# A fused RWKV attention and mixing kernel: the first batch's MLP in runs of three and six steps, with new places for late weights and for the second batch's preparation

## The chip, the cores and the metric

The kernel runs on one core of one Trainium2 chip. The metric is the device time of one launch, in microseconds (us). The kernel before took 422.9 us, the median of three runs (422.41 to 423.47). The engines are called by the profile's names: PE (TensorE), DVE (VectorE), ACT (ScalarE), POOL (GpSimd) and SP (SyncE, which issues most DMAs here).

## The reference

The first half is a linear attention with a decaying state, for 4 batches and 8 heads over 768 tokens of 48 numbers each. The second half mixes over tokens (rank 32) and then over channels (384 to 1536 and back).

```python
for t in range(S):                                   # attention, per batch and head
    cur = einsum('bhd,bhe->bhde', u * k[t], v[t])
    y[t] = einsum('bhd,bhde->bhe', r[t], state + cur)
    state = w * state + einsum('bhd,bhe->bhde', k[t], v[t])
x = y.transpose(0, 2, 1, 3).reshape(4, 768, 384)
h = x.transpose(0, 2, 1) @ U @ V                     # U: 768 x 32, V: 32 x 768
u = x + h.transpose(0, 2, 1)
out = u + maximum(u @ w_ch1, 0) @ w_ch2              # w_ch1: 384 x 1536, w_ch2: 1536 x 384
```

U, V, w_ch1 and w_ch2 arrive as float64 and are turned into float32 on the chip, bit by bit. Each 32-bit factor of the MLP is then split into a high part (a cast to the fp32r type) and a low part (what the cast lost), and a product is three matmuls: high by high, low by high, high by low.

## The kernel before, in words

**Attention by chunks.** The four batches of 768 tokens are 24 chunks of 128 tokens, six to a batch: n = 0 to 5 are batch 0, 6 to 11 batch 1, and so on. A chunk needs its r, k, v (loads `ld`, `vsw`; for some chunks of batches 1 to 3 `bl`, blocks of r and k in pieces of 128 bytes, line 686), then `ks`, transposes with decay factors (`rT`, `kT`), `dv` and `dg` (r times k times u, and its sum), which together are called its preparation. Then it goes through PE (`pab`, `pav`) and the carried state (`S`, `SW`), and line 896 adds the result up as `x_n`, a tile of 128 tokens by 384 channels.

**G and u^T.** G = U^T x needs all six x of a batch. For batch 0 it is gathered in the PSUM bank `wake` (`c_gx`), and `c_g0` copies it to SBUF: the high part by ACT (`Gs_0`, line 951), the low part by DVE (line 952). Then u, transposed, is made in two blocks of 384 tokens (t = 0 and 1) by `c_xu`: PE transposes x into banks `pu` and adds V^T G; ACT casts the high part `uTh` (line 1034), DVE subtracts the low part `uTl` (line 1035).

**The MLP by steps.** A step (t, f) is one token block and one of 12 slices of 128 hidden channels. `m_1` multiplies u^T by slice f of W1 (nine matmuls into bank `mm`, of which there is one); ACT makes relu and cast (`hr`, line 1103, and `hh`), an engine the low part (`hl`, line 1105). `m_2` multiplies by slice f of W2 (nine matmuls into three banks `acc`, one for each 128 tokens, called `p2`). The half steps go m_1 of step i, then m_2 of step i - 1. The first step of a block with f = 0 puts three "gates" ahead (`p<-Gs,V`: G by V, the part of u that is not x). At the end of a run of steps with one t, DVE adds the three `p2` to the x tiles (line 1143), which frees the banks for the next run; once all 12 slices are added, x is stored. Batch 0 goes through three runs before the change: t 0 with f 0 to 5, t 1 with f 0 to 11, t 0 with f 6 to 11. The other batches have two: t 0 and t 1 with all 12.

**The weights.** Every slice of W1 or W2 is a "unit" (`w1_f`, `w2_f`): a load of 384 KB (line 512, on SP), a byte instruction that picks out the upper exponent bits (line 533 on DVE or 537 on ACT), a scaling on ACT (line 559), sign and join on DVE (lines 540 and 543), the high part on ACT (line 577) and the low part on POOL or DVE (line 578). Batch 0 decodes them all; the results stay for the other batches.

**The order.** A planner in the kernel (`Plan`) writes the order of every engine's queue. Each operation has a due time (its key, given by `at(t, ...)`), an estimated cost, what it reads and writes (`Buf`), and rings of buffers by tag. The planner goes forward in estimated time, gives an engine the operation with the earliest key of those that it thinks ready, and chooses between engines where an operation has alternatives. On the chip each engine then works its queue in that order; waits are put in by the real reads and writes. In gaps that the planner foresees on PE it puts filler matmuls (`wake`, `wake2`). Due times are set by constants: `T0` = 46 (the start of batch 0's MLP in the planner's time), `PER` = 1.95 a half step, `FRONT` = 9 and `EACH` = 5.5 for the chunks of batch 0, `LEAD` = 12 (how long before its use a weight is loaded), `EARLY` = 4 (weights loaded ahead of the rest).

## Time and profile before

| | before |
|---|---|
| median of three runs | 422.9 us (422.41 to 423.47) |
| the profiled execution | 422.63 us, of which the span is 420.9 us |
| mean granted clock of PE | 0.991 |
| PE busy | 402.0 us (96%) |
| PE weight loads | 388.6 us (92%) |
| DVE busy | 280.6 us (67%) |
| ACT busy | 188.1 us (45%) |
| POOL busy | 75.6 us (18%) |
| HBM read, written | 37.95 MB, 8.26 MB |

The span runs from the first to the last instruction of the profiled execution, and all positions below are microseconds from its start. Busy is the time with an instruction in work. A row of a timeline shows the start, how long the group took, the engine, the line, the operation, its tiles and shape and how many instructions stand in it; a bracket at its end gives an idle time ahead of it and what ended it. A row of the stretches shows the stretch and its length, then for PE, PE's weight loads, DVE, ACT and POOL the busy time and in brackets the instructions, then the granted clock of PE (1.00 is full speed), the share of time in which the DMA engines worked and the rate in GB/s.

### The profile page before, as it was taken

The numbers are of one execution on the slowest core, as the hardware profiler recorded it, in microseconds if no ns is written. First come the engines' busy times: TensorE is split into PE (matmuls) and PEld (weight loads), VectorE is DVE, ScalarE is ACT, GpSimd is POOL, SyncE is SP. The second block draws the span as 40 slices with busy tenths as digits, with TensorE's granted clock in tenths as the row PEclk, the third lists the DMA queues.
The fourth block names the chain that finished last, engine by engine and source line by source line (L and its number), as shares of the span: only waits on it lengthen the run. The fifth ranks groups of instructions, "written<-read, shape, count | busy, mean of one in ns | idle before, by whom it ended". The sixth has DMA issues, their size and how long they took to land.

```text
span 420.9 us, 12333 instructions
## 1 busy us (share of the span) xinstructions
PE 402.0 (96%) x5111; PEld 388.6 (92%) x5111; DVE 280.6 (67%) x620; ACT 188.1 (45%) x482; POOL 75.6 (18%) x111
## 2 busy tenths in 40 slices
PE   7798679999999999999999999999999999999994
PEld 7698569999999999999999999999999999999994
...
GB/s 135 151 160 205 277 204 153 185 256 155 104 144 121 179 91 179 111 157 154 83 106 125 117 166 79 152 90 80 58 2 2 59 111 0 2 0 59 0 2 61
DMA packets 199521, 47.09 MB, mean 112 GB/s; under 512 B 183073, under 2 KB 197922, under 8 KB 199458
## 3 DMA queue, kind: packets, MB, share of 16 engines
q1 hardware_dynamic: 194274, 44.75, 52.4%
q10 hardware_dynamic: 5184, 1.48, 2.0%
q8 instruction: 42, 0.69, 0.7%
...
HBM read 37.95 MB, written 8.26 MB: 110 GB/s over the span
## 4 chain that ended last, share of the span: by engine, by line
PE 84%; DVE 5%; DMA 4%; ACT 3%; issue 1%; SPq 1%; ACTq 1%; DVEq 0%
PE p L341 70%; PE pab L784 3%; PE pav L822 3%; DMA vsw<-in_v_dram 3%; PE pav L828 2%; PE pab L799 2%; PE wake L341 1%; DMA raw_w<-in_moe_w_ch_dram 1%; SPq L653 1%; PE pG L962 1%; DVE raw_w L540 1%; ACT raw_w L537 1%; DVE uTl L1031 1%; ACTq L665 1%; PE ptk L746 1%
## 5 line engine op out<-in xcount | busy, mean ns | idle before, releaser
L341 PE MATMUL p<-uTh,w1s 128*128 128x384 f32 x576 | 148.3, 338 | 1.1 <-ACT hr L1103 1.0
L1105 DVE TENSOR_TENSOR hl<-hr,hh 128x384 fp32r<-128x384 f32 x92 | 53.2, 579 | 111.2 <-ACT hh L1104 104.9
L1103 ACT ACTIVATE hr<-p 128x384 f32<-128x384 f32 x96 | 47.1, 491 | 179.0 <-PE p L341 176.7
L341 PE MATMUL p<-w2s,hh 128*128 128x384 f32 x576 | 118.1, 337 | 0.0
L341 PEld LDWEIGHTS p<-uTh,w1s 128*128 128x128 f32 x576 | 103.4, 188 | 2.6 <-ACT hr L1103 1.9
L341 PEld LDWEIGHTS p<-w2s,hh 128*128 128x128 f32 x576 | 100.5, 188 | 1.0 <-ACT hh L1104 0.2
L341 PE MATMUL p<-uTl,w1s 128*128 128x384 f32 x288 | 96.4, 335 | 0.0
L341 PE MATMUL p<-w2s,hl 128*128 128x384 f32 x288 | 65.9, 335 | 0.0
L341 PEld LDWEIGHTS p<-uTl,w1s 128*128 128x128 f32 x288 | 54.2, 188 | 0.0
L341 PEld LDWEIGHTS p<-w2s,hl 128*128 128x128 f32 x288 | 51.3, 188 | 0.0
L1104 ACT CAST hh<-hr 128x384 fp32r<-128x384 f32 x96 | 49.2, 513 | 2.6
L716 ACT ACTIVATE dv<-ldv,dg 128x48 f32<-128x48 f32 x104 | 25.2, 325 | 3.9 <-DVE dg L712 3.6
L696 POOL MEMSET ks<- 128x128 f32 x24 | 4.9, 205 | 89.2 <-PE pab L799 80.6
L784 PEld LDWEIGHTS pab<-rT,kT 48*64 48x64 f32 x768 | 13.4, 134 | 7.9 <-issue 4.2
L784 PE MATMUL pab<-rT,kT 48*64 48x64 f32 x768 | 16.7, 224 | 2.4 <-ACT tab L461 1.2
L341 PE MATMUL wake<-ident 128*128 128x128 f32 x116 | 17.2, 307 | 1.7 <-POOL ident masks.py:199 1.7
L889 DVE TENSOR_TENSOR am<-pab,mask 128x256 f32<-128x256 f32 x48 | 18.0, 414 | 0.0
L341 PEld LDWEIGHTS wake<-ident 128*128 128x128 f32 x116 | 16.2, 221 | 1.7 <-POOL ident masks.py:199 1.7
L822 PE MATMUL pav<-vsw,am 64*64 64x48 f32 x384 | 17.2, 220 | 0.5 <-issue 0.5
L822 PE MATMUL pav<-ldv,am 64*64 64x48 f32 x384 | 17.2, 220 | 0.0
L930 ACT ACTIVATE SW<-S,wm 112x48 f32<-112x48 f32 x56 | 14.2, 323 | 6.7 <-DVE S L917 5.0
L917 DVE TENSOR_TENSOR S<-pab,SW 112x192 f32<-112x192 f32 x40 | 14.0, 351 | 3.8 <-PE pab L799 3.4
...
## 6 DMA issues: line engine op xcount, KB each, us to landing
...
```

Source lines behind the costliest of these rows:

```text
L341: return nc.tensor.matmul(*args, **kw)
L716: nc.scalar.activation(dv.t[:, h], vt()[:, h], AF.Copy, scale=dg.t[:, h:h + 1])
L784: return [lambda q=q, i=i: nc.tensor.matmul(pt.t[(i ^ j) * C2:(i ^ j) * C2 + C2, q * C2:(q + 1) * C2], lhsT=kT.t[rows, q, i * C2:(i + 1) * ...
L799: return nc.tensor.matmul(pt.t[j * HP:j * HP + m, SU + q * D:SU + (q + 1) * D], lhsT=ks.t[half, 2 * q + j, :m], rhs=vt()[half, 2 * q + j, ...
L822: return nc.tensor.matmul(to(q, j, i), lhsT=am[j].t[half, q, :], rhs=vsw[n].t[half, q, :] if j else vt()[half, 2 * q, :], start=(q == 0), ...
L828: return nc.tensor.matmul(to(q, row, i), lhsT=rT.t[rows, q, i * C2:(i + 1) * C2], rhs=St[n, i].t[rows, q, :], start=False, stop=(q == NP - ...
L889: on_dve(256, lambda e: e.tensor_tensor(am.t, abs_[n][j].t[:, :SU].rearrange("p (h t) -> p h t", h=NP), mask_.unsqueeze(1).broadcast_to([1 ...
L917: on_dve(192, lambda e, new=new, ptv=ptv, dec=decayed[n, j]: e.tensor_tensor(new.t, ptv(), dec.t, ALU.add), [new], [pt, decayed[n, j]])
L930: nc.scalar.activation(dec.t[:, q], new.t[:, q], AF.Copy, scale=wm.t[:, q])
L1103: on_act(384, lambda: nc.scalar.activation(hr.t, pt.t[:, :TB], AF.Relu), [hr], [pt])
L1104: on_act(384, lambda: nc.scalar.copy(hh.t, hr.t), [hh], [hr])
L1105: on_either(384, lambda e: e.tensor_tensor(hl.t, hr.t, f32(hh.t), ALU.subtract), [hl], [hr, hh])
```

## The change

Four things are edited.

- **Runs.** Batch 0's MLP changes its token block more often (`ZIG` = 3): t 0 with f 0 to 2, t 1 with f 0 to 5, t 0 with f 3 to 8, t 1 with f 6 to 11, t 0 with f 9 to 11. The steps and their matmuls are the same 24. Five runs end where three did, each with three adds of `p2` to x, so batch 0 has 15 of these adds where it had 9. `step(f)`, from which the due times of the weights are worked out, follows the new runs: slices 3 and later are first used later than they were.
- **Marks for the planner.** While `behind(mark, ...)` records operations, each one that is neither a DMA nor PE's gets `mark` as something it reads. The mark is no memory and makes no wait on the chip; it keeps the planner from placing the operation ahead of the mark's writer. `g_done` is written by the low part of `Gs_0`: all weight units behind the first five (u, v, w1_0, w2_0, w1_1) are decoded behind it. `u_done` is written by the low parts of u^T's block 0: the preparation of the chunks of batches 1 to 3 is put behind it.
- **Buffers.** There are 12 buffers for x tiles instead of 11. The start-up table `tw` takes a buffer of the ring `bl` instead of `hh`.
- **Dead code.** `by_bank`, `BANKS` and the parameter `tag` of `unit`, which are not used with the values before, are taken out. The diff below leaves this part out.

```diff
@@ -72,6 +72,7 @@
         self.woken = []
         self.work = {}
         self.clocks = {}
+        self.behind = None
 
     def op(self, eng, ns, fn, w=(), r=(), alt=(), lock=False, dma=0.0, rows=0, late=0.0, tiled=False, dk=0.0):
 
@@ -79,6 +80,8 @@
         if self.direct:
             fn()
             return None
+        if self.behind is not None and not dma and eng != "PE":
+            r = [*r, self.behind]
         o = Op()
         o.n = len(self.ops)
         o.key = (self.key + dk, o.n)
...
@@ -304,7 +307,7 @@
     TB = 384
     NTB = S // TB
     TPB = TB // 128
-    NX = 11
+    NX = 12
     NXS = 4
     NH = 4
     NR = 2
...
@@ -447,7 +450,7 @@
         on_dve(4, lambda e: e.tensor_copy(tt[:, 1, :, C2:C2 + 1], top(1)), [tabT], [sq])
         on_dve(4, lambda e: e.tensor_mul(wm.t, top(0), top(0)), [wm], [sq])
 
-        tw = xbuf([PD, NP, C], F32, "hh", NH, "tw")
+        tw = xbuf([PD, NP, C], F32, "bl", 5, "tw")
         on_dve(512, lambda e: e.tensor_mul(subs(tw.t), table(1), wm.t.unsqueeze(2).broadcast_to([PD, NP, 2, C2])), [tw],
                [wm, tabT], port=True)
...
@@ -936,6 +928,16 @@
     Gs = {}
     uT = {}
 
+
+    g_done = Buf(const, [1, 1], F32, None, 1, "g_done")
+    u_done = Buf(const, [1, 1], F32, None, 1, "u_done")
+
+    def behind(mark, fn):
+
+        plan.behind = mark
+        fn()
+        plan.behind = None
+
     def c_gx(n):
 
...
@@ -949,7 +951,7 @@
             return wk.t[:3 * R, 128:]
         G = Gs[0] = wbuf([3 * R, DM], F32R, "Gs", 1, "Gs_0")
         on_act(384, lambda: nc.scalar.copy(G.t, pt()), [G], [(wk, "g")])
-        on_dve(384, lambda e: e.tensor_tensor(G.t[R:2 * R], pt()[R:2 * R], f32(G.t[R:2 * R]), ALU.subtract), [G], [(wk, "g")])
+        on_dve(384, lambda e: e.tensor_tensor(G.t[R:2 * R], pt()[R:2 * R], f32(G.t[R:2 * R]), ALU.subtract), [G, g_done], [(wk, "g")])
 
     def c_g(b):
...
@@ -1033,7 +1035,8 @@
                 continue
             on_act(384, lambda ct=ct, pt=pt: nc.scalar.copy(uh.t[:, ct, :], pt.t[:, :TB]), [(uh, ct)], [pt])
             on_dve(384, lambda e, ct=ct, pt=pt: e.tensor_tensor(ul.t[:, ct, :], pt.t[:, :TB], f32(uh.t[:, ct, :]),
-                                                                ALU.subtract), [(ul, ct)], [pt, (uh, ct)])
+                                                                ALU.subtract), [(ul, ct)] + ([] if t else [(u_done, ct)]),
+                   [pt, (uh, ct)])
 
     def c_ut(b, i):
...
@@ -1151,11 +1154,20 @@
     left = {}
     stored = []
 
+    ZIG = 3
+
+    def zigzag():
+
+        runs = [(0, 0, ZIG)]
+        for f in range(0, NFT, ZIG):
+            t = 1 - runs[-1][0]
+            runs.append((t, f, min(f + 2 * ZIG, NFT) if t else min(f + 2 * ZIG, NFT)))
+        return runs
+
     def mlp_units(b):
 
 
-        H_ = NFT // 2
-        runs = ([(0, 0, H_), (1, 0, NFT), (0, H_, NFT)] if b == 0 and NTB == 2 else [(t, 0, NFT) for t in range(NTB)])
+        runs = zigzag() if b == 0 and NTB == 2 else [(t, 0, NFT) for t in range(NTB)]
         steps = [(t, f, f == f0, (f1 - f0) if f == f1 - 1 else 0) for t, f0, f1 in runs for f in range(f0, f1)]
         units = []
...
@@ -1253,6 +1265,8 @@
     T0, PER = 46.0, 1.95
     EARLY, LEAD = 4, 12.0
     FRONT, EACH = 9.0, 5.5
+    DONE = FRONT + NCH * EACH
+    SOON = 3
     for p in pav:
         at(-101, lambda p=p: on_dve(512, lambda e: e.memset(p.t, 0.0), [p], []))
...
@@ -1271,18 +1285,21 @@
 
     def step(f):
 
-        return f + (NFT // 2 if f >= NFT // 2 else 0)
+        return f + ZIG * (f // ZIG)
     for f in range(NFT):
         use += [2 * step(f) - (f > 0), 2 * step(f) + 2]
     for i, (load, convert) in enumerate(wu):
 
         at(-84.9 + 0.01 * i if i < 2 else -50 + 0.1 * i if i < 2 + EARLY else T0 + use[i] * PER - 6 - LEAD, load)
-        at((T0 + use[i] * PER - 6 if i > 1 else -14 + T0) + 0.01 * i, convert)
+        if i < 2 + SOON:
+            at((T0 + use[i] * PER - 6 if i > 1 else -14 + T0) + 0.01 * i, convert)
+        else:
+            at(max(T0 + use[i] * PER - 6, DONE + 0.1) + 0.01 * i, lambda c=convert: behind(g_done, c))
 
     def prepare(n, t):
         fs = [lambda: a_ks(n), lambda: a_tr(n, 1), lambda: a_tr(n, 0), lambda: a_dv(n)]
         for i, f in enumerate(fs[1:3] + fs[:1] + fs[3:] if n == 0 else fs):
-            at(t + 0.2 * i, f)
+            at(t + 0.2 * i, f if n < NCH else lambda f=f: behind(u_done, f))
 
     def attention(b, t0, per, lead, step):
         n0 = b * NCH
@@ -1296,7 +1313,7 @@
             if front(n + 4):
 
                 at(t + per / 2 + 0.01, lambda n=n: a_load_odd(n + 4, -100.0))
-            at(t - 0.1, lambda n=n: a_dg(n))
+            at(t - 0.1, lambda n=n: a_dg(n) if n < NCH else behind(u_done, lambda: a_dg(n)))
             if b == 0:
                 at(max(t + (1.53 if c == NCH - 2 else 1) * per - 0.05, 36.6 + 0.01 * c), lambda n=n: gx.append(c_gx(n)))
         return t0 + per * NCH
```

The order of the queues moves at these places. DVE, around the end of chunk 5 (its `x_5`) and G's low part (`Gs_0`), before:

```order
L896 TENSOR_TENSOR x_5_1024<-pav1_98,x_5_1024 128x384
L712 TENSOR_REDUCE dg_6_1045<-dv_6_953 128x8
L543 SCALAR_TENSOR_TENSOR raw_w2_0_700<-raw_w2_0_700 128x384
L540 SCALAR_TENSOR_TENSOR raw_w1_2_852<-raw_w1_2_852 128x384
L540 SCALAR_TENSOR_TENSOR raw_w2_1_832<-raw_w2_1_832 128x384
L543 SCALAR_TENSOR_TENSOR raw_w1_2_852<-raw_w1_2_852 128x384
L543 SCALAR_TENSOR_TENSOR raw_w2_1_832<-raw_w2_1_832 128x384
L540 SCALAR_TENSOR_TENSOR raw_w1_3_858<-raw_w1_3_858 128x384
L952 TENSOR_TENSOR Gs_0_1068<-wake_93,Gs_0_1068 32x384
L578 TENSOR_TENSOR w2s_0_1070<-raw_w2_0_700,w2s_0_1070 128x384
```

DVE at the same place, with the change:

```order
L888 TENSOR_TENSOR x_5_1008<-pav1_98,x_5_1008 128x384
L546 SCALAR_TENSOR_TENSOR raw_w2_0_702<-raw_w2_0_702 128x384
L570 TENSOR_TENSOR w2s_0_1030<-raw_w2_0_702,w2s_0_1030 128x384
L954 TENSOR_TENSOR Gs_0_1035<-wake_93,Gs_0_1035 32x384
L536 TENSOR_SCALAR raw_w1_2_850<-raw_w1_2_850 128x384
L536 TENSOR_SCALAR raw_w2_1_830<-raw_w2_1_830 128x384
L536 TENSOR_SCALAR raw_w2_2_856<-raw_w2_2_856 128x384
```

The sum `dg` of chunk 6 and six decoding instructions stood between x_5 and G's low part, of which five belong to w1_2, w2_1 and w1_3. Now one join and the low part of w2_0 stand there, and the decoding of later weights begins behind G.

ACT, around its cast of G, before:

```order
L577 CAST w1s_1_1030<-raw_w1_1_710 128x384
L559 ACTIVATE raw_w1_3_858<-raw_w1_3_858 128x384
L716 ACTIVATE dv_6_953<-ldv_6_807,dg_6_1045 128x48 x8
L951 CAST Gs_0_1068<-wake_93 96x384
L577 CAST w2s_0_1070<-raw_w2_0_700 128x384
L537 ACTIVATE raw_w2_2_961<-raw_w2_2_961 128x384
L577 CAST w1s_2_1078<-raw_w1_2_852 128x384
```

ACT at the same place, with the change:

```order
L569 CAST w2s_0_1030<-raw_w2_0_702 128x384
L953 CAST Gs_0_1035<-wake_93 96x384
L553 ACTIVATE raw_w1_2_850<-raw_w1_2_850 128x384
L553 ACTIVATE raw_w2_1_830<-raw_w2_1_830 128x384
L1036 CAST uTh_0_0_1054<-pu0_0_0_953 128x384
L1036 CAST uTh_0_0_1054<-pu0_0_1_962 128x384
L1036 CAST uTh_0_0_1054<-pu0_0_2_1014 128x384
```

Eight `dv` pieces of chunk 6 and the scaling of w1_3 stood ahead of G's cast; now they are gone from there, and two scalings stand between it and the casts of u^T.

SP, which issues the loads, from the raw weights behind those of the start, before:

```order
L512 DMA raw_w2_2_961<-in_moe_w_ch2_dram 128x768
L512 DMA raw_w1_4_1010<-in_moe_w_ch1_dram 128x3x256
L653 DMA ldv_7_1016<-in_v_dram 128x8x48
L665 DMA vsw_7_1026<-in_v_dram 64x4x48
L512 DMA raw_w2_3_1038<-in_moe_w_ch2_dram 128x768
L665 DMA vsw_7_1026<-in_v_dram 64x4x48
L653 DMA ldk_8_1014<-in_k_dram 128x8x48
L653 DMA ldv_8_1064<-in_v_dram 128x8x48
L512 DMA raw_w1_5_1075<-in_moe_w_ch1_dram 128x3x256
L512 DMA raw_w2_4_1086<-in_moe_w_ch2_dram 128x768
L665 DMA vsw_8_1094<-in_v_dram 64x4x48 x2
L686 DMA bl_9_0_1115<-in_r_dram 32x12x32 x4
```

SP with the change, down to the loads of the same weights:

```order
L657 DMA vsw_7_1002<-in_v_dram 64x4x48 x2
L645 DMA ldv_8_1022<-in_v_dram 128x8x48
L657 DMA vsw_8_1026<-in_v_dram 64x4x48 x2
L678 DMA bl_9_0_1039<-in_r_dram 32x12x32 x7
L515 DMA raw_w1_3_1103<-in_moe_w_ch1_dram 128x3x256
L678 DMA bl_9_0_1039<-in_r_dram 32x12x32
L678 DMA bl_9_1_1119<-in_k_dram 32x12x32 x4
L645 DMA ldk_8_1155<-in_k_dram 128x8x48
L678 DMA bl_9_1_1119<-in_k_dram 32x12x32
L515 DMA raw_w1_4_1182<-in_moe_w_ch1_dram 128x3x256
L515 DMA raw_w2_3_1190<-in_moe_w_ch2_dram 128x768
```

The weights w1_4 and w2_3 stood ahead of the first block load (`bl`) and stand behind several of them now; w1_3 does too.

DVE at the end of batch 0's first run of steps, where it adds `p2` to the x tiles 0 to 2, before (after six steps):

```order
L543 SCALAR_TENSOR_TENSOR raw_w1_6_1296<-raw_w1_6_1296 128x384
L540 SCALAR_TENSOR_TENSOR raw_w1_7_1303<-raw_w1_7_1303 128x384
L543 SCALAR_TENSOR_TENSOR raw_w1_7_1303<-raw_w1_7_1303 128x384
L1105 TENSOR_TENSOR hl_0_0_5_1375<-hr_0_0_5_1363,hh_0_0_5_1370 128x384
L1105 TENSOR_TENSOR hl_0_1_0_1407<-hr_0_1_0_1393,hh_0_1_0_1401 128x384
L1143 TENSOR_TENSOR x_0_411<-p2_0_0_1105,x_0_411 128x384
L1143 TENSOR_TENSOR x_1_540<-p2_1_0_1112,x_1_540 128x384
L1143 TENSOR_TENSOR x_2_675<-p2_2_0_1118,x_2_675 128x384
```

The same with the change (after three steps):

```order
L1108 TENSOR_TENSOR hl_0_0_2_1216<-hr_0_0_2_1201,hh_0_0_2_1209 128x384
L704 TENSOR_REDUCE dg_6_1223<-dv_6_1136 128x8
L704 TENSOR_REDUCE dg_7_1228<-dv_7_1180 128x8
L536 TENSOR_SCALAR raw_w1_4_1182<-raw_w1_4_1182 128x384
L714 TENSOR_TENSOR dv_6_1136<-ldv_6_805,dg_6_1223 128x384
L543 SCALAR_TENSOR_TENSOR raw_w1_4_1182<-raw_w1_4_1182 128x384
L570 TENSOR_TENSOR w1s_3_1242<-raw_w1_3_1103,w1s_3_1242 128x384
L546 SCALAR_TENSOR_TENSOR raw_w1_4_1182<-raw_w1_4_1182 128x384
L1146 TENSOR_TENSOR x_0_409<-p2_0_0_1072,x_0_409 128x384
L1146 TENSOR_TENSOR x_1_540<-p2_1_0_1076,x_1_540 128x384
L1146 TENSOR_TENSOR x_2_676<-p2_2_0_1081,x_2_676 128x384
```

Ahead of the three adds stood the decoding of w1_6 and w1_7 and two `hl`; now it is the decoding of w1_4, the low part of w1_3 and `dg` and `dv` of batch 1's first chunks.

More of the change, by code (lines that the diff above doesn't have):

```diff
@@ L487, in rwkv_moe, with unit @@
     landing = []
-    def unit(name, shape, parts, split, tag=None):
+    def unit(name, shape, parts, split):
         P_ = shape[0]
@@ L543, in join @@
             nc.vector.scalar_tensor_tensor(word(0), word(1), 3, word(0), ALU.logical_shift_left, ALU.bitwise_or)
-        def by_bank():
-            pt = bank(tag, f"top_{name}")
-            on_act(n, lambda: nc.scalar.activation(pt.t[:P_, :n], word(1).bitcast(F32), AF.Copy, scale=2.0 ** -112), [pt], loaded)
-            for s_, o_ in ((-2 ** 31, ALU.bitwise_and), (3, ALU.logical_shift_left)):
-                op("DVE", dve(n), lambda s_=s_, o_=o_: nc.vector.scalar_tensor_tensor(
-                    word(0), pt.t[:P_, :n].bitcast(I32), s_, word(0), o_, ALU.bitwise_or), [(raw, "lo")], [pt])
         def convert():
@@ L555, in convert @@
                    alt=[("ACT", act(n) + 100, on_act_byte, False)])
[L556 to L558 removed]
+            if wide:
                 on_act(n, lambda: nc.scalar.activation(word(1).bitcast(F32), word(1).bitcast(F32), AF.Copy,
```

12 lines of the change are left out of this document (4 added, 8 removed).

## The prediction

> **What bounds the kernel now.** The page's first part and the busy time by stretch come first.
>
> ```profile
> span 420.9 us, 12333 instructions
> PE 402.0 (96%) x5111; PEld 388.6 (92%) x5111; DVE 280.6 (67%) x620; ACT 188.1 (45%) x482; POOL 75.6 (18%) x111
> ```
>
> ```profile
> 47.37:53.61 6.24, 1.17 (x10) 0.88 (x9) 6.21 (x8) 4.50 (x14) 4.76 (x4) 0.84 1.01 267
> 53.61:61.84 8.23, 6.62 (x27) 5.81 (x27) 7.46 (x16) 6.54 (x17) 0.00 (x0) 0.71 0.93 220
> 61.84:70.00 8.16, 8.16 (x45) 7.85 (x46) 8.16 (x18) 7.26 (x19) 1.03 (x1) 1.00 0.64 99
> 70.00:80.00 10.00, 10.00 (x60) 10.00 (x59) 4.79 (x10) 5.82 (x15) 0.00 (x0) 1.00 0.95 204
> 80.00:100.00 20.00, 20.00 (x280) 19.19 (x279) 17.96 (x41) 16.05 (x43) 6.17 (x8) 1.00 0.84 223
> 100.00:120.00 20.00, 19.63 (x460) 18.64 (x459) 20.00 (x47) 13.31 (x41) 9.83 (x11) 1.00 0.66 117
> 120.00:146.00 26.00, 26.00 (x349) 25.00 (x347) 25.19 (x54) 11.70 (x34) 6.74 (x9) 1.00 0.73 146
> ```
>
> The columns are the stretch, its length, then busy time of PE, PE weight load, DVE, ACT and POOL, the granted clock, the DMA share and GB/s. From 61.84 us on PE does not stop: 0.37 us are missing in the next 84. The change leaves the matmuls as they are, so the end moves by what PE no longer loses before 61.84, less what it newly loses behind it. The timeline of PE shows the first.
>
> ```profile
> 48.16 0.38 PE L341 MATMUL pu<-ident,x 128*128 128x128 f32 x2
> 54.22 0.79 PE L341 MATMUL wake<-V 96*128 96x512 f32 x1 [5.68 <-DVE Gs L952]
> 54.81 1.80 PE L341 MATMUL pu<-V,Gs 96*128 96x384 f32 x5
> 56.83 1.27 PE L341 MATMUL p<-Gs,V 96*128 96x384 f32 x3
> 57.91 0.74 PE L341 MATMUL p<-uTh,w1s 128*128 128x384 f32 x2
> 60.23 0.60 PE L746 MATMUL ptk<-ident,ks 128*128 128x128 f32 x4
> 61.84 0.44 PE L341 MATMUL p<-uTh,w1s 128*128 128x384 f32 x1 [1.01 <-ACT hr L1103]
> ```
>
> PE stands for 5.68 us until DVE has G. Then come five products with G (pu) and three gates (p<-Gs), step 0's first half (from 57.91) and a wait of 1.01 us for the relu. What DVE and ACT did meanwhile:
>
> ```profile
> 46.82 0.55 DVE L896 TENSOR_TENSOR x<-pav,x 128x384 f32<-128x384 f32 x1
> 47.74 1.07 DVE L543 SCALAR_TENSOR_TENSOR raw_w<-raw_w 128x384 int32<-128x384 int32 x1
> 48.74 2.64 DVE L540 SCALAR_TENSOR_TENSOR raw_w<-raw_w 128x384 int32<-128x384 int32 x2
> 51.30 1.81 DVE L543 SCALAR_TENSOR_TENSOR raw_w<-raw_w 128x384 int32<-128x384 int32 x2
> 53.61 0.55 DVE L952 TENSOR_TENSOR Gs<-wake,Gs 32x384 fp32r<-32x384 f32 x1
> 55.88 2.13 DVE L1035 TENSOR_TENSOR uTl<-pu,uTh 128x384 fp32r<-128x384 f32 x4 [0.66 <-ACT uTh L1034]
> ```
>
> ```profile
> 47.86 1.91 ACT L716 ACTIVATE dv<-ldv,dg 128x48 f32<-128x48 f32 x8
> 49.68 0.46 ACT L951 CAST Gs<-wake 96x384 fp32r<-96x384 f32 x1
> 55.37 1.24 ACT L1034 CAST uTh<-pu 128x384 fp32r<-128x384 f32 x3 [1.69 <-PE pu L341]
> 57.67 0.58 ACT L537 ACTIVATE raw_w<-raw_w 128x384 int32<-128x384 uint8 x1
> 60.83 0.58 ACT L537 ACTIVATE raw_w<-raw_w 128x384 int32<-128x384 uint8 x1
> 61.27 0.52 ACT L1103 ACTIVATE hr<-p 128x384 f32<-128x384 f32 x1
> ```
>
> The chunk that completes batch 0 (x_5) ends at 47.37. The low part of G starts only at 53.61, since batch 1's dg and six decoding instructions stand ahead of it on DVE; five of these take 5.5 us between 47.74 and 53.11 while POOL works beside them. On ACT eight dv pieces stand ahead of G's cast, and eight pieces of weight decoding run between u^T and the first relu (57.67 to 61.27).
>
> **The change, part by part.** I go along the path to the second step's first matmul, which was at 61.84. Paces: a DVE instruction of 384 columns follows the last after 0.47 us ((1.48 - 0.56)/2 in the row below rounds to that), an ACT cast after 0.37 ((1.24 - 0.50)/2), a full-clock matmul of 384 columns after 0.179 (19.29/108).
>
> ```profile
> 81.15 1.48 DVE L1143 TENSOR_TENSOR x<-p,x 128x384 f32<-128x384 f32 x3
> 82.99 0.69 PE L341 MATMUL p<-Gs,V 96*128 96x384 f32 x3
> 61.84 19.29 PE p L341 x108
> ```
>
> *Up to x_5.* DVE has as many instructions ahead of x_5's two adds as before, but w1s_0's low part goes to POOL (1.02 us by the row below) and pushes that engine's ks_6 and dv_6 back to about 45.3. The join of w1_1, due on DVE at 44.74, then runs beside POOL. One such join beside POOL took 1.07 instead of 0.55 us (47.74). I take +0.4, with bounds 0 (no overlap) and 0.6 (POOL's whole rest): x_5 at 47.8.
>
> ```profile
> 47.38 1.02 POOL L578 TENSOR_TENSOR w1s<-raw_w,w1s 128x384 fp32r<-128x384 f32 x1 [2.92 <-ACT w1s L577]
> ```
>
> *To G.* Behind x_5 DVE now has the join of w2_0 (to 48.3) and then, after ACT's w2s_0 cast (48.8), that weight's low part (to 49.3); ACT casts G behind w2s_0 by 49.2. So G's low part runs from 49.3 to 49.85, against 54.16: 4.3 us gained. POOL has nothing left at that place. The dg, dv_6 and the decoding of the later weights stand behind.
>
> *G to step 1.* PE: refill 0.25, first pu 0.18, 0.2 to the reader: 50.5. ACT has finished two scalings by then and casts five uTh at 0.37, to 52.4. DVE first does three byte instructions (0.27 each) and two signs, to 51.6, then three uTl, to 53.0; gates to 53.2, step 0's nine matmuls (1.6) to 54.8, pu's last block (0.5) and ptk (0.45) to 55.7; relu 55.0 to 55.5. Step 1 begins at 55.7. That stretch was 61.84 - 54.16 = 7.7 us and is now 5.85, another 1.85 us. About half of it is clock:
>
> ```profile
> 36.00:38.00 2.00, 0.73 (x7) 0.62 (x7) 1.73 (x5) 2.00 (x9) 0.71 (x2) 1.00 1.15 308
> 38.00:40.00 2.00, 2.00 (x43) 1.85 (x45) 0.66 (x3) 1.22 (x4) 0.00 (x0) 1.00 0.44 93
> 50.00:52.00 2.00, 0.00 (x0) 0.00 (x0) 2.00 (x3) 1.03 (x3) 1.92 (x2) 0.89 1.16 269
> 54.00:56.00 2.00, 1.78 (x5) 1.69 (x6) 1.31 (x4) 0.64 (x2) 0.00 (x0) 0.50 1.05 293
> ```
>
> The 5.68 us of waiting ended with a clock of 0.50, under which the five pu took 0.36 us each. PE now stands about 1.3 us (from 48.5 to 49.85); the 1.27 us that it stood between 36 and 38 left the clock at 1.00. If it fell none the less, pu, gates and the planner's four refills would take 2 us more. Head start: 61.84 - 55.7 = 6.1 us.
>
> *Run switches and DVE.* Five runs end where three did: 15 adds of p2 to x instead of 9, six more at 0.47. At a switch three adds must end within one half step of PE (1.6 us); at 81.15 they took 1.48 and PE's gates followed at 82.99 with no wait. The first switch now comes after three steps: from 55.7 PE does six half steps to 65.4, one more, and reaches the gates at 67.0. DVE ends step 0's hl at 57.15 (two joins, two uTl, two low parts, a sign, a uTl and this hl at 0.47 from 53.0); then 17 instructions (16 at 0.47 and one byte, among them batch 1's dv, ks and two dg) bring it to 64.95, and the three adds, the first of which must wait for its bank until 65.2, to 66.6. That is 0.4 us of room; the other switches have more, since attention matmuls or pG stand at them. In all, DVE has 196 instructions between G and batch 1's G copy, where it had 182: six adds (2.8), five sign or join (2.35), five byte (1.35), five dv (2.35), less four transposes (1.6), two kT, one rT, one hl (2.2) and a little: +5.3 us. Idle of DVE from 53.61 to 146 was 0.77 + 0 + 5.21 + 2.04 + 0 + 0.81 = 8.8 us, by the stretches above. The new window is 1.8 us shorter, so 1.7 us of idle remain. I take 0.5 us given back (0 if every result is early enough, 7 if DVE must idle as before: a rival).
>
> *Loads.* On SP w1_3, w1_4, w2_3 now stand behind 7 to 13 of the block loads (bl).
>
> ```profile
> 58.15 3.17 SPq L686 DMA_DIRECT2D bl<-in_r_dram  x4
> 61.37 4.26 SPq L686 DMA_DIRECT2D bl<-in_k_dram  x8
> DMA to landing us min/median/max: 4.0/4.6/6.3
> 62.00:64.00 2.00, 2.00 (x12) 2.00 (x13) 2.00 (x5) 2.00 (x6) 0.46 (x1) 1.00 0.58 90
> ```
>
> SP reaches 48.5 with the ldv and vsw of chunks 7 and 8; a bl takes it 0.53 us (4.26/8) to 0.79 (3.17/4). w1_3 is issued at 52.2 to 54.0 and w1_4 at 56.5 to 60; with the 4.6 us to land (the median of the raw weights between 25 and 62) that is 57 to 59 and 61 to 64.6. DVE wants w1_4 at 62.8. I take the short end: on time. The long end, 1.8 us late, less the 0.4 of room, makes the first switch 1.4 us late. [...] The stretch 62 to 64, where bl alone were issued, had a DMA share of only 0.58, which speaks for the short end.
>
> The twelfth x buffer and tw's move cost no instruction; their cover is that x_11 would else wait for a stored x of batch 0.
>
> Sum: -4.3 (G) - 1.85 (G to step 1) + 0.5 = -5.65 us. The profiled execution took 422.63 us (span 420.9 and 1.7 around it), so 417.0; the median of the runs is 0.3 higher, so **417.2**.
>
> **Rivals.** (1) *DVE binds in part.* For it: 1.7 us of idle left in 91. Against it: hl is wanted some 4 us after its matmuls, so a late one is not yet a wait. If half of the old idle must stay, 4.4 - 1.7 = 2.7 us are lost in place of the 0.5 counted: 419.4. (2) *DVE binds wholly, the other side.* DVE works in order, and each idle spell that it needs (5.21 us between 70 and 80 were waits for ACT and PE) is pushed on to PE once the room is gone: 8.8 - 1.7 = 7.1 us lost in place of 0.5: 423.8. It decides from 7.9 us of kept idle on, where the loss (7.9 - 1.7) is the whole gain. Against it: at the same count of steps the paces bring DVE to the first attention of batch 1 no later than PE. (3) *Late weights*, the long ends above with the longest landing (6.3 us was seen for these loads): w1_4 at 66.3, 3.5 us late at its byte instruction, with the adds and so the gates behind it on an engine that works in order: 3.1 us more, 420.3. Against it: the share of 0.58. (4) *The marks do little*: they order the plan only and put no wait on the chip. If G ends 2 us later than worked out, the clock falls as well, and 5.65 - 2 - 2 leave 1.65 us: 421.2. Against it: nothing of length is left ahead of G on either engine.
>
> **How the numbers follow.** Forecast 0.58 (own range 415.8 to 418.6: all idle harmless and the old 0.37 us gone, or 1.4 us more lost); rival 1 0.16, rival 3 0.08, rival 4 0.08, rival 2 0.10. The range 415.6 to 420.8 leaves out rivals 2 and 4. A difference of 0.3% (1.3 us, the border at 421.6) is about what can be told from none. Faster holds the forecast, rivals 1 and 3 and a quarter of 4, which lies near the border (0.84); same the rest of 4 and a fifth of 2 (0.08); slower the rest of 2 (0.08).
>
> **What would show it.** In the new profile: G's low part on DVE ending between 49.4 and 50.5; a granted clock of 1.00 in every stretch from 50 to 60; no spell of PE over 1.5 us between 48 and 55; the second step's first matmul near 55.7; PE full from there on to the end, above all at the gates near 67 and from 75 to 140, where DVE should show under 2 us of idle. A wait of PE for the x adds or for a raw_w load there, or p waiting for hl, would give the rivals right. It is wrong if G stays behind 52, or if PE misses more than 3 us after its start.

## The result, and the profile after

With the change the kernel takes 417.94 us (median of four runs, 416.80 to 418.57) where the kernel before took 422.65 in the runs beside it: a ratio of 0.9882, with a 95% interval of 0.9854 to 0.9910. The forecast was 417.2, its own range 415.8 to 418.6. The profiled execution took 418.57 us, the slowest of the four. A profile shows one execution, and single runs of one kernel lie 1.4 to 7 us apart. The ratios leave out a run that is over 1.5% above the fastest of its kernel, which is one (425.83 us) of run 8. The page of the profiled execution begins:

```profile
span 416.9 us, 12303 instructions
PE 401.8 (96%) x5112; PEld 387.0 (93%) x5112; DVE 285.4 (68%) x642; ACT 178.7 (43%) x445; POOL 63.7 (15%) x106
```

PE is as busy as before (402.0 us); the span is 4.0 us shorter. The busy time by stretch follows, over the stretches that were shown of the kernel before (the columns are the same):

```profile
47.37:53.61 6.24, 4.69 (x22) 3.38 (x23) 5.53 (x14) 4.30 (x10) 0.00 (x0) 1.00 0.66 119
53.61:61.84 8.23, 8.23 (x52) 8.19 (x51) 7.91 (x18) 6.70 (x16) 0.00 (x0) 1.00 0.78 140
61.84:70.00 8.16, 8.16 (x48) 8.01 (x47) 7.96 (x18) 6.39 (x20) 1.02 (x1) 1.00 1.08 272
70.00:80.00 10.00, 9.51 (x57) 9.11 (x56) 6.78 (x15) 5.65 (x14) 0.21 (x1) 1.00 0.77 143
80.00:100.00 20.00, 19.41 (x385) 17.54 (x383) 19.37 (x44) 15.38 (x39) 8.09 (x10) 1.00 0.86 194
100.00:120.00 20.00, 20.00 (x350) 19.02 (x344) 20.00 (x46) 12.01 (x34) 4.92 (x9) 1.00 0.79 181
120.00:146.00 26.00, 25.65 (x343) 24.08 (x341) 25.83 (x57) 11.97 (x28) 9.02 (x10) 1.00 0.74 147
```

In the first two stretches PE gained 3.52 and 1.61 us of work, and the granted clock, 0.84 and 0.71 before, is 1.00. From 70 to 146 PE now misses 0.49, 0.59 and 0.35 us where it missed 0, 0.37 (between 100 and 120) and 0: the gain at the start is partly given back. The timeline of PE shows the start:

```profile
47.62 0.90 PE L344 MATMUL wake<-x,Uf 128*96 128x128 f32 x6 [0.41 <-DVE x L888]
49.84 0.49 PE L344 MATMUL wake<-V 96*128 96x512 f32 x1 [1.10 <-DVE Gs L954]
50.17 1.04 PE L344 MATMUL pu<-V,Gs 96*128 96x384 f32 x5
52.29 1.37 PE L344 MATMUL p<-Gs,V 96*128 96x384 f32 x3
53.50 0.51 PE L344 MATMUL p<-uTh,w1s 128*128 128x384 f32 x2
55.92 0.60 PE L344 MATMUL p<-uTh,w1s 128*128 128x384 f32 x2
66.96 0.79 PE L344 MATMUL p<-Gs,V 96*128 96x384 f32 x3
```

PE waits 1.10 us for G instead of 5.68, the five pu take 1.04 us where they took 1.80, the second step begins at 55.92 instead of 61.84, and the gates of the first run switch (66.96) follow without a wait. DVE at the same place:

```profile
47.02 0.55 DVE L888 TENSOR_TENSOR x<-pav,x 128x384 f32<-128x384 f32 x1
47.49 0.55 DVE L546 SCALAR_TENSOR_TENSOR raw_w<-raw_w 128x384 int32<-128x384 int32 x1
48.65 0.56 DVE L570 TENSOR_TENSOR w2s<-raw_w,w2s 128x384 fp32r<-128x384 f32 x1 [0.61 <-ACT w2s L569]
49.23 0.55 DVE L954 TENSOR_TENSOR Gs<-wake,Gs 32x384 fp32r<-32x384 f32 x1
```

x_5 ends at 47.57, and the low part of G at 49.78 instead of 54.16. What was given back stands further on. DVE's timeline there:

```profile
63.62 0.36 DVE L536 TENSOR_SCALAR raw_w<-raw_w 128x384 int32<-128x384 uint8 x1 [0.15 <-DMA raw_w<-in_moe_w_ch_dram]
71.56 0.36 DVE L536 TENSOR_SCALAR raw_w<-raw_w 128x384 int32<-128x384 uint8 x1 [1.57 <-DMA raw_w<-in_moe_w_ch_dram]
71.84 0.55 DVE L1108 TENSOR_TENSOR hl<-hr,hh 128x384 fp32r<-128x384 f32 x1
79.26 0.36 DVE L536 TENSOR_SCALAR raw_w<-raw_w 128x384 int32<-128x384 uint8 x1 [1.24 <-DMA raw_w<-in_moe_w_ch_dram]
```

and PE's:

```profile
72.44 0.80 PE L344 MATMUL p<-w2s,hl 128*128 128x384 f32 x3 [0.49 <-DVE hl L1108]
84.94 0.69 PE L776 MATMUL pab<-rT,kT 48*64 48x64 f32 x32 [0.54 <-DVE rT L747]
```

DVE stands 1.57 us for a weight's load; the hl behind it comes late, and PE waits 0.49 us. After a second stand of 1.24 us, DVE's rT comes 0.54 us late for the first attention of batch 1.

### The profile page after: what moved, and what is told of

It reads as the page before. It is cut to its first block, busy times and chain, and to the rows that moved or that the text cites. A ratio compares the mean times of both kernels' runs of the same rounds, so it can differ in the third digit from the quotient of the medians.

```text
span 416.9 us, 12303 instructions
## 1 busy us (share of the span) xinstructions
PE 401.8 (96%) x5112; PEld 387.0 (93%) x5112; DVE 285.4 (68%) x642; ACT 178.7 (43%) x445; POOL 63.7 (15%) x106
## 4 chain that ended last, share of the span: by engine, by line
PE 70%; DVE 12%; DMA 8%; SPq 4%; ACT 3%; issue 2%; ACTq 1%; DVEq 0%
PE p L344 58%; DMA raw_w<-in_moe_w_ch_dram 4%; PE pab L776 2%; SPq L678 2%; PE pav L814 2%; DMA vsw<-in_v_dram 2%; PE pav L820 2%; PE pab L791 2%; DMA ldv<-in_v_dram 2%; DVE raw_w L546 1%; DVE raw_w L543 1%; DVE hl L1108 1%; DVE x L888 1%; PE wake L344 1%; SPq L515 1%
## 5 line engine op out<-in xcount | busy, mean ns | idle before, releaser
L1108 DVE TENSOR_TENSOR hl<-hr,hh 128x384 fp32r<-128x384 f32 x90 | 50.7, 564 | 103.9 <-ACT hh L1107 102.4
L708 ACT ACTIVATE dv<-ldv,dg 128x48 f32<-128x48 f32 x88 | 21.3, 325 | 4.7 <-DVE dg L704 4.7
L1146 DVE TENSOR_TENSOR x<-p,x 128x384 f32<-128x384 f32 x33 | 16.3, 545 | 3.1 <-PE p L344 3.1
L918 POOL TENSOR_TENSOR SW<-S,wm 112x192 f32<-112x192 f32 x24 | 12.2, 508 | 29.0 <-DVE S L909 27.5
```

The source lines that it names most:

```text
L708: nc.scalar.activation(dv.t[:, h], vt()[:, h], AF.Copy, scale=dg.t[:, h:h + 1])
L918: e.tensor_mul(dec.t, new.t, wm.t.broadcast_to([PD, NP, D]))
L1108: on_either(384, lambda e: e.tensor_tensor(hl.t, hr.t, f32(hh.t), ALU.subtract), [hl], [hr, hh])
L1146: on_dve(384, lambda e, x=x, pt=pt: e.tensor_tensor(x.t, pt.t[:, :DM], x.t, ALU.add), [x], [pt])
```

## The experiments

**1. Marks and buffers, without the short runs.**

```diff
-        runs = zigzag() if b == 0 and NTB == 2 else [(t, 0, NFT) for t in range(NTB)]
+        H_ = NFT // 2
+        runs = ([(0, 0, H_), (1, 0, NFT), (0, H_, NFT)] if b == 0 and NTB == 2 else [(t, 0, NFT) for t in range(NTB)])
...
-        return f + ZIG * (f // ZIG)
+        return f + (NFT // 2 if f >= NFT // 2 else 0)
```

> The marks, the twelfth x buffer and tw's place as in the change; batch 0's runs and the due times of the weights as before (6, 12 and 6 steps). Theory A (the gain is the head start at G, which comes from what no longer stands ahead of G on DVE and ACT; the short runs only make room for it): G's low part still ends near 49.8 us and the second step begins near 56. Behind it DVE has 52 instructions instead of 34 before the first adds of p2 to x, about 24.4 us at 0.47, so it reaches them near 75 us, and PE reaches its gates near 77: nearly in balance, with single steps late. 418 to 420.5 us. Rival B (without the short runs the late weights hold PE, since a step of PE takes 3.15 us and the decoding of one slice with its hl takes DVE up to 3.8): waits of PE for w1s or w2s between 62 and 77 that eat most of the head start, 421 us or more.

Measured: 418.55 us, a ratio of 0.9878 (0.9834 to 0.9922), the same as the change. Theory A holds and rival B falls. The waits of PE in its profile, from 47.8 us on (engine, line, what it waited for, us in total, times, the longest):

```profile
PE wake L344 <- DVE Gs L954: 1.2, 1, 1.2
PE wake L344 <- DVE x L888: 1.0, 1, 1.0
PE pu L344 <- DVE Gs L978: 0.4, 1, 0.4
```

PE's timeline, at the products with G:

```profile
51.64 1.80 PE L344 MATMUL pu<-V,Gs 96*128 96x384 f32 x5
```

No weight and no hl is waited for. From G (50.99) to the second step (59.03) it takes 8.0 us, with the five pu at 0.36 us each as before the change, since the clock fell (0.50 from 50.6 to 57.4 us); behind it PE misses only the 0.4 us at batch 1's G. So the second step begins 3.1 us later than in the change, and the time is the same none the less: in these two profiles the change loses 2.6 us of the 3.1 again behind the second step (361.0 us to the end of the span, against 358.4).

**2. The short runs and the buffers, without the marks.**

```diff
-            at(max(T0 + use[i] * PER - 6, DONE + 0.1) + 0.01 * i, lambda c=convert: behind(g_done, c))
+            at(T0 + use[i] * PER - 6 + 0.01 * i, convert)
...
-            at(t + 0.2 * i, f if n < NCH else lambda f=f: behind(u_done, f))
+            at(t + 0.2 * i, f)
...
-            at(t - 0.1, lambda n=n: a_dg(n) if n < NCH else behind(u_done, lambda: a_dg(n)))
+            at(t - 0.1, lambda n=n: a_dg(n))
```

> The runs of 3 and 6 steps with the due times that follow from them, without either mark; buffers as in the change. Between x_5 and G's low part DVE then has four instructions (a low part, two joins or signs of early weights, one of w1_2) instead of seven before and two in the change. Theory A: G's low part ends 1 to 2 us later than in the change (50.7 to 51.8), the second step begins that much later (57 to 58), and half to four fifths of the gain is there: 418.5 to 420.5 us. Rival B (the runs alone bring nothing, since the order ahead of G comes from the marks): G ends behind 53 us, 421.5 us or more. Rival C (the runs alone do all): within 0.5 us of the change.

Measured: 420.48 us, a ratio of 0.9932 (0.9911 to 0.9953), six tenths of the gain: theory A, against B and C. The later due times alone clear part of the place ahead of G: four DVE instructions stand there, and G's low part ends 3.26 us behind x_5, against 2.21 with the marks (and 6.79 before). In this execution x_5 happened to end at 46.40, so G came at 49.66, earlier than expected; but PE had waited 2.15 us, the clock fell to 0.50 from 49.4 to 56.2 us, and the second step began at 59.15, 9.5 us behind G. PE's timeline there:

```profile
49.72 0.80 PE L344 MATMUL wake<-V 96*128 96x512 f32 x1 [2.15 <-DVE Gs L954]
51.91 4.45 PE L344 MATMUL wake<-V 96*128 96x512 f32 x10
```

The clock is not all of these 9.5 us. Ten fillers stand ahead of the gates, 4.45 us long, where the change has four of 1.09 us in all: without the marks, dg and dv of batch 1 and parts of later weights stand ahead of uTl on DVE (its first three start at 53.09, 3.4 us behind G, in the change 1.9). That the planner put in the fillers for that is argued, not shown.

**3. G later by nine subtractions in place of one.**

```diff
-        on_dve(384, lambda e: e.tensor_tensor(G.t[R:2 * R], pt()[R:2 * R], f32(G.t[R:2 * R]), ALU.subtract), [G, g_done], [(wk, "g")])
+        def low(e):
+            for _ in range(9):
+                e.tensor_tensor(G.t[R:2 * R], pt()[R:2 * R], f32(G.t[R:2 * R]), ALU.subtract)
+        on_dve(384, low, [G, g_done], [(wk, "g")])
```

> The change, with G's low part subtracted nine times in a row on DVE (the same numbers come out), every queue otherwise in the same order. By the pace of 0.47 us G is done 3.8 us later, near 53.6. If the clock falls after a long wait of PE as in the profile before (0.50 after 5.68 us), PE waits 4.9 us, the five pu, the refills and the gates run at half clock, and the second step begins 5 to 6 us later than with the change, at 61 to 62: 422.5 to 424 us. Rival: the clock has no part, the second step begins 3.8 us later, near 59.7, and DVE, which is 3.8 us behind as well, gives nothing back: 421 to 422 us. If PE had slack behind G, less than 3.8 us would be lost: under 421.

Measured: 424.22 us, a ratio of 1.0009 (0.9981 to 1.0037): the whole gain is gone. The timeline of DVE and PE:

```profile
51.27 5.23 DVE L957 TENSOR_TENSOR Gs<-wake,Gs 32x384 fp32r<-32x384 f32 x9
...
56.64 0.77 PE L344 MATMUL wake<-V 96*128 96x512 f32 x1 [5.88 <-DVE Gs L957]
57.21 1.80 PE L344 MATMUL pu<-V,Gs 96*128 96x384 f32 x5
```

The stretch behind the wait began at this clock:

```profile
54.00:56.00 2.00, 0.00 (x0) 0.00 (x0) 1.86 (x5) 0.00 (x0) 0.00 (x0) 0.50 0.63 77
```

The nine took 5.23 us, 0.9 more than at the pace of 0.47, PE waited 5.88 us, and the clock was 0.50, with pu at 0.36 us as in the kernel before. From G to the second step (64.70) it took 8.2 us instead of 6.1: 2.1 us of clock. Another 2.0 us of this execution are older than the edit: x_5 ended at 49.59, since PE had stood 1.83 us at 40.4 and the clock was 0.76 between 40 and 47, on a queue that is the change's own up to there. The rival without the clock (421 to 422) falls by what the trace shows, the clock of 0.50 and the 8.2 us behind G; the time alone would not settle it, since it may hold such older losses too.

**4. Weights loaded earlier.**

```diff
-    EARLY, LEAD = 4, 12.0
+    EARLY, LEAD = 4, 20.0
```

> The change with weights loaded 20 instead of 12 of the planner's us ahead of use (LEAD), so eight weights instead of six are issued ahead of the first block load of batch 1; DVE then meets loaded weights. Theory: the 2.1 us given back behind G's head start come in good part from DVE standing for a late weight (1.57, 1.24 and 0.15 us), behind which hl and rT came late for PE (0.49 and 0.54 us); these waits go, 0.7 to 1.3 us are gained against the change: 416.6 to 417.3 us. Rival: DVE has no slack anyway and binds, so the time stays within 0.4 us of the change (417.5 to 418.4). Rival on the other side: the earlier weight loads push back v, k and the block loads of batch 1, and G or batch 1's attention comes later: over 418.5.

Measured: 418.93 us, a ratio of 0.9892 (0.9851 to 0.9933), no gain. DVE's waits between 53 and 146 us name no load any more:

```profile
DVE hl L1108 <- ACT hh L1107: 1.2, 2, 1.0
DVE w2s L570 <- ACT w2s L569: 1.0, 2, 0.8
DVE x L888 <- PE pav L820: 0.6, 1, 0.6
```

So the stands for late weights went as expected, and from the second step (57.86) to the end of the span it takes 359.2 us instead of 361.0. But x_5 came at 49.05, with a clock of 0.76 between 40 and 47 after a wait of PE of 2.06 us. Whether the eight earlier loads did that or chance (the run before had it without them) isn't settled; in the time the two cancel. The number, 418.93, lies where the rival on the other side had put it (over 418.5, with G later); by the interval it can't be told from the change.

**5. DVE relieved of 21 sign instructions.**

```diff
         def sign():
+            if name not in ("u", "v", "w1_0", "w2_0", "w1_1"):
+                nc.vector.tensor_scalar(raw.t[:P_, :1], raw.t[:P_, :1], 0, 0, ALU.bitwise_or, ALU.bitwise_or)
+                return
```

> The change without the sign instruction of the 21 weight units that are decoded behind G (their signs are left out, so the MLP's numbers are other ones); in each one's place stands an instruction on one column, and every queue keeps its order. DVE has about 21 x 0.4 = 8.4 us less to do between 50 and 140 us. Theory (what was given back behind G comes from weights that land late, DVE itself has room): the stands of DVE for raw_w stay or get longer, the time stays within 0.6 us of the change, 417.3 to 418.5 us. Rival (DVE binds there): PE's waits for hl, rT and G's low part go and 1.5 us or more are gained, under 416.5 us.

Measured: 417.03 us, a ratio of 0.9860 (0.9825 to 0.9895), between the two expectations and not to be told from the change. The stretch from G to the end of batch 0, of the change and of this run:

```profile
49.80:146.00 96.20, 94.52 (x1233) 88.46 (x1233) 91.62 (x202) 60.66 (x154) 23.24 (x29) 1.00 0.81 172
```
```profile
49.80:146.00 96.20, 95.19 (x1244) 90.42 (x1245) 85.70 (x207) 61.98 (x161) 23.20 (x30) 1.00 0.81 176
```

DVE lost 5.9 us of busy time net, and PE gained 0.67 us. DVE stands as long for late weights as in the change (3.3 us, there 3.0, in three waits each, from 50 us on). So DVE's load does not bind behind G; in these two executions it was worth 0.7 us.

**6. The buffers undone.**

```diff
-    NX = 12
+    NX = 11
...
-        tw = xbuf([PD, NP, C], F32, "bl", 5, "tw")
+        tw = xbuf([PD, NP, C], F32, "hh", NH, "tw")
```

> The change with its third part undone: 11 x buffers and tw in the ring hh, as before. Theory (that part costs and brings nothing): 417.3 to 418.6 us. Rival: chunk 11 waits for an x buffer of batch 0 that is freed only with the last run, since the short runs finish all of batch 0's tiles late; PE then waits at batch 1's attention or at its G, over 419 us.

Measured: 422.36 us, a ratio of 0.9997 (0.9972 to 1.0023). The whole gain is gone, which speaks for the rival. The start is the change's (G at 49.77, the second step at 55.94); the loss is at batch 1's G. The timeline of DVE (the last add of x_11) and PE:

```profile
144.82 0.56 DVE L888 TENSOR_TENSOR x<-pav,x 128x384 f32<-128x384 f32 x1
...
144.88 1.20 PE L964 MATMUL pG<-x,Uf 128*32 128x96 f32 x48
149.46 0.59 PE L344 MATMUL pu<-V,Gs 96*128 96x384 f32 x2 [1.27 <-DVE Gs L978]
150.54 0.45 PE L344 MATMUL p<-Gs,V 96*128 96x384 f32 x1 [0.49 <-DVE x L1146]
```

and the stretch with the clock:

```profile
150.00:160.00 10.00, 9.39 (x37) 7.46 (x37) 6.80 (x14) 5.08 (x15) 0.00 (x0) 0.83 0.69 141
```

In the change that add starts at 136.19 and G's matmuls (pG) at 141.32, with two half steps of batch 0 between them and the first use of G. With 11 buffers pG comes at 144.88, and only the last eleven matmuls of batch 0 are left to cover the making of G: PE waits 1.27 and 0.49 us, and the clock falls (0.83 between 150 and 160). This profile took 420.98 us, 2.4 us more than the first of the change; by the ratios the loss is 4.9 us, so only half of it is seen here.

**7. Only w1_0 decoded ahead of G.**

```diff
-    SOON = 3
+    SOON = 1
```

> The change with SOON at 1: w2_0 and w1_1 are decoded behind G like the others, only w1_0 (and u, v) ahead. In the profiles so far DVE stands 1.0 to 2.6 us for a weight's load at 37.9 to 39.9 us, with chunk 4's S behind it, and x_5 is early or late with it (46.4 with the earliest landing, 48.65 with the latest). Theory: only two instructions on w1_0 are left there and nothing between x_5 and G's low part, so x_5 ends 0.7 to 1.7 us earlier (46 to 47) and G's low part 2 to 3 us earlier (47 to 48); the second step, which needs w1_1, begins 1 to 2.5 us earlier; if half of that is given back behind it, 416.5 to 417.4 us. Rival: what bounds the time behind G is the decoding, not G, and the end stays: 417.5 to 418.5 us. Rival on the other side: w1_1 or w2_0 comes late, PE stands and its clock falls, over 418.6 us.

Measured: 422.14 us, a ratio of 0.9990 (0.9959 to 1.0021), single runs from 419.35 to 425.01. My theory falls. x_5 ended at 47.04 and G at 49.09, 0.7 us earlier and not 2 to 3; ACT could cast G only when PE had added x_5 to it (timeline of ACT):

```profile
48.03 0.47 ACT L953 CAST Gs<-wake 96x384 fp32r<-96x384 f32 x1 [4.13 <-PE wake L344]
```

The longest entry among PE's waits behind that:

```profile
PE p L344 <- ACT hr L1106: 1.6, 2, 1.0
```

The second step, which needs w1_1, began at 56.08, no earlier, and PE missed 3.4 us behind G instead of 1.6, half of it for relus, the rest at batch 1's G. That is the rival on the other side in its sign, not in its mechanism (the clock stayed at 1.00 from 48 to 56), and it explains the profile's 420.25 us. The median is 1.9 us above that; where the other executions lose it, and what makes them so unlike, stays open.

**8. The same with the long runs.** Edits 1 and 7 together.

> As the run before (SOON at 1), with batch 0's runs of 6, 12 and 6 steps as before the change. From the second step to the end PE took 355.6 us in the change and 352.8 with the long runs and the marks. Theory: that difference belongs to the short runs (six more adds on DVE and weight loads that stand behind block loads), so with the earlier G this kernel is the fastest: 415.5 to 417 us. Rival: a later start is what made those 352.8 us short (loads had more time), and an earlier G is given back: 417.5 to 419 us.

Measured: 421.64 us, a ratio of 0.9965 (0.9932 to 0.9998), single runs from 418.88 to 425.83. The rival's outcome, and more: the theory falls. From the second step (58.50) to the end of the span this profile took 363.6 us, where run 1 took 358.4. Part of these 5.2 us may be clock again: the granted clock over the whole execution was 0.987, where run 4, with the same 0.76 between 40 and 47 us, had 0.992. That is about 2 us more (0.005 of 422, an estimate), and not between 48 and 58 us, where the clock was 1.00. PE also waited 1.2 us for a relu and 0.4 us for rT. This execution is also one of the slower ones (423.89 us). So the long runs don't make this decoding order cheap; why it is dear stays open.

**9. The change again,** unaltered, beside runs 10 to 12.

> The change as it is, beside the runs that follow and on their chip. Theory: the gain is that of its first four runs, a ratio to the kernel before of 0.985 to 0.991 (417 to 418.5 us). Rival: those four runs were lucky, since whether PE's clock falls near 42 and 50 us depends on when a weight lands (37.9 to 39.9 us in the profiles): single runs up to 422 us and a ratio of 0.992 or more.

Measured: 416.72 us, a ratio of 0.9846 (0.9815 to 0.9877); of six runs one was over 417.2. The theory holds. Its profile took 416.58 us, and the page begins:

```profile
span 414.9 us, 12303 instructions
```

The timeline of PE and of DVE:

```profile
49.35 0.50 PE L344 MATMUL wake<-V 96*128 96x512 f32 x1 [1.11 <-DVE Gs L954]
55.44 0.59 PE L344 MATMUL p<-uTh,w1s 128*128 128x384 f32 x2
...
69.67 0.36 DVE L536 TENSOR_SCALAR raw_w<-raw_w 128x384 int32<-128x384 uint8 x1 [0.55 <-DMA raw_w<-in_moe_w_ch_dram]
77.75 0.36 DVE L536 TENSOR_SCALAR raw_w<-raw_w 128x384 int32<-128x384 uint8 x1 [1.58 <-DMA raw_w<-in_moe_w_ch_dram]
```

G ends at 49.29, the second step begins at 55.44, DVE still stands for the same two loads, but until 69.67 and 77.75 instead of 71.56 and 79.26, and PE has no wait over 0.15 us between 56 and 128. The whole program is 0.5 us ahead of the first profile here, the landings are 1.5 to 1.9, and PE waited for neither the hl nor the rT behind them.

**10. The marks alone.** The kernel before with the marks: edits 1 and 6 together.

> The kernel before with the two marks and nothing else of the change: runs of 6, 12 and 6 steps, 11 x buffers, tw in the ring hh. Theory: the twelfth buffer is needed only by the short runs (with them batch 0's last x tiles are finished three steps later, and chunk 11 gets its buffer late, which made the run with the old buffers lose all its gain at batch 1's G), so the marks alone give what marks and buffers gave: 417.5 to 419.5 us, a ratio of 0.985 to 0.992. Rival: the twelfth buffer gives something of its own, the time is over 420.5 us, with PE waiting near batch 1's G (143 to 152 us).

Measured: 418.25 us, a ratio of 0.9875 (0.9845 to 0.9904). The theory holds: with the long runs the twelfth buffer brings nothing, and the marks alone bring what the change brings, within the intervals. Beside each other the change (run 9) was 1.5 us faster, five of its six runs below all six of this one; in the first batches the two kernels with marks lay 0.6 us apart (417.94 and 418.55). So short runs and buffers together may bring a little on top, which these runs don't settle.

**11. Marks, long runs and fillers on PE ahead of x_5.** Edit 1, and:

```diff
-            o = pe(225, lambda i=i: whole(wk.t[:3 * R, 128 * (i + 1):128 * (i + 2)], lhsT=Uf.t[:, n].rearrange("p k r -> p (k r)"),
+            o = pe(225, lambda i=i: ([fill() for _ in range(8 if n == NCH - 1 and i == 0 else 0)],
+                                     whole(wk.t[:3 * R, 128 * (i + 1):128 * (i + 2)], lhsT=Uf.t[:, n].rearrange("p k r -> p (k r)"),
...
```

> Marks and buffers of the change, batch 0's runs as before (6, 12, 6), and eight more filler matmuls (128 columns, about 0.11 us each) on PE ahead of the three that add x_5 to G, where PE stood 1.02 us for x_5; every queue is otherwise that of the run with the marks and the long runs. There the clock fell to 0.50 at 51 us after two waits of 1.02 and 1.22 us, and from G to the second step it took 8.0 us, where it takes 6.1 to 6.2 at full clock. Theory (the two waits together bring the clock down): it stays at 1.00 from 48 to 58, the second step begins 6.0 to 6.5 us behind G, and 1 to 2 us are gained against that run: 416.5 to 417.8 us, the fastest of all. Rival: the clock falls none the less, for the wait for G alone, and nothing is gained (418 to 419.5). Rival on the other side: PE reaches G earlier than is of use, and what is gained there is given back behind it: 418 to 419 us at full clock.

Measured: 417.45 us, a ratio of 0.9868 (0.9826 to 0.9911); not to be told from runs 1 and 10 in the time. The trace shows two matmuls for each filler, 22 of them (`wake<-ident`, 2.62 us) where run 1 has 6. In the profile the mechanism is there: PE's wait before G in the timeline, and the stretch behind it.

```profile
51.83 0.51 PE L344 MATMUL wake<-V 96*128 96x512 f32 x1 [0.93 <-DVE Gs L955]
```
```profile
54.00:56.00 2.00, 1.81 (x7) 1.17 (x7) 2.00 (x5) 1.78 (x5) 0.00 (x0) 1.00 0.83 200
```

The same two views of run 10, which has no fillers:

```profile
49.09 0.90 PE L344 MATMUL wake<-x,Uf 128*96 128x128 f32 x6 [0.92 <-DVE x L888]
51.75 0.74 PE L344 MATMUL wake<-V 96*128 96x512 f32 x1 [1.54 <-DVE Gs L954]
```
```profile
54.00:56.00 2.00, 2.00 (x7) 1.62 (x6) 2.00 (x6) 2.00 (x6) 0.00 (x0) 0.50 0.82 201
```

PE waits only for G, the clock stays at 1.00, and from G to the second step it takes 6.2 us instead of 8.3. But from there to the end of the span it takes 358.9 us instead of 358.2, so a third of that is given back (the last rival, in part). The 2.0 us of clock show at the second step, then, but not in the time.

**12. The buffers alone,** in the kernel before (edit 6 the other way round).

> The kernel before with the twelfth x buffer and tw's new place alone. Theory: nothing waits for an x buffer there, so it stays within 0.3% of the kernel before (421.6 to 424). Rival: the buffers bring part of the gain by themselves: under 421 us.

Measured: 423.85 us, a ratio of 1.0001 (0.9974 to 1.0027), as expected.

Taken together, with each part of the change in or out (ratios to the kernel before):

| runs of 3 and 6 | marks | buffers | ratio |
|---|---|---|---|
| no | no | yes | 1.0001 (0.9974 to 1.0027) |
| no | yes | no | 0.9875 (0.9845 to 0.9904) |
| no | yes | yes | 0.9878 (0.9834 to 0.9922) |
| yes | no | yes | 0.9932 (0.9911 to 0.9953) |
| yes | yes | no | 0.9997 (0.9972 to 1.0023) |
| yes | yes | yes | 0.9882 (0.9854 to 0.9910), again 0.9846 (0.9815 to 0.9877) |

No version was found that beats the change clearly.

## Why the prediction was right, point by point

| | predicted | profile after | the change again |
|---|---|---|---|
| x_5 ends | 47.8 us | 47.57 | 47.07 |
| G's low part ends | 49.85 | 49.78 | 49.29 |
| G to the second step | 5.85 | 6.14 | 6.15 |
| second step begins | 55.7 | 55.92 | 55.44 |
| gates of the first switch | 67.0 | 66.96 | 66.47 |
| given back behind the second step | 0.5 | 1.9 | 0.4 |
| profiled execution | 417.0 | 418.57 | 416.58 |
| median | 417.2 | 417.94 | 416.72 |

*Up to G.* That x_5 ended within 0.3 us of the forecast is partly luck: over all profiles it ended between 46.40 and 49.59 us. The step from x_5 to G held: nothing but w2_0's join and low part stood between, and 2.21 us passed where 2.05 were worked out. But it was hardly these two that took the time, as the prediction has it: in run 7, without them, 2.04 us passed, for PE's adding of x_5 to G, ACT's cast (from 48.03 on) and the low part itself. Run 3 shows that this is the path: G later by 4.7 us behind x_5, with the clock that fell behind it, took the whole gain away. Runs 1, 2 and 10 show what gave it: the marks fully, the due times that come with the short runs in part. The two marks were not taken apart.

*G to step 1, half of it clock.* Held, and shown apart: the stretch took 6.1 to 6.2 us at full clock (the change twice, runs 4, 6 and 11) and 7.9 to 9.5 at a fallen one (runs 1, 2, 3, 10 and 12). The cleanest pair is runs 11 and 10, 6.2 and 8.3 us, which is the 2 us that the prediction gave for a fall; run 2's 9.5 has more fillers besides, and runs 7 and 8, which decode w2_0 and w1_1 there, took 7.0 and 7.7 us at full clock. What is not shown is that the clock counts in the whole time: runs 1 and 10 began the second step late, at a fallen clock, and gained as much as the change.

*Run switches and DVE.* The first switch was as tight as worked out and cost nothing. The 0.5 us given back was the term that was mis-sized for the first profile: 1.9 us, by the spans (416.9 - 55.92 = 361.0 against 420.9 - 61.84 = 359.1), of which 1.3 us are waits of PE (1.6, where it waited 0.4 before); the rest is not traced. The cause is not DVE's load, as rivals 1 and 2 had it: 5.9 us less of it brought PE 0.67 us (run 5). By runs 4 and 9 it is rival 3 in small: late weights, with hl and rT behind them on DVE. DVE's idle time between 75 and 140 us was 2.3 us (1.9 in run 9), where under 2 were expected.

*Loads.* "On time" was wrong by little at the place named. SP issued w1_3 and the group with w1_4 here:

```profile
54.19 0.47 SPq L515 DMA_DIRECT2D raw_w<-in_moe_w_ch_dram  x1
60.12 1.93 SPq L515 DMA_DIRECT2D raw_w<-in_moe_w_ch_dram  x3
```

w1_3 went out 0.2 us behind the end of my bracket and w1_4's group at its end (60); DVE stood 0.15 us for w1_4 (63.62) and not at all at the switch, but 1.57 and 1.24 us for the next two. SP took 0.53 us for each of the seven block loads ahead of w1_3 (3.68/7, from 50.46 us on), which is the pace of the bracket's short end. The long end, at 0.79 us each, with 1.4 us more lost and so 418.6, came near the first profile by chance: it put the 1.4 us at the first switch, where nothing was lost, and w1_4, which it had 1.8 us late, was 0.15 us late. It lies 1.9 us above the second median.

*Marks do little* (rival 4) was wrong: the marks, which only the planner sees, kept both engines clear, and with no other edit they carry the gain (run 10).

*The twelfth buffer.* The prediction named its cover and gave it no price, because the kernel before had no wait there. That is true of the kernel before (run 12) and of the marks (run 10), but with the short runs the buffer is worth the whole gain (run 6): batch 0's tiles of block 1 are finished by its fourth run instead of its second, chunk 11 gets its buffer late, and batch 1's G loses the matmuls that cover it. That it is the x buffer and not tw's place is read from where x_11's add stands; neither was undone without the other.
